# Token shift kept in a ring buffer, both mixes on VectorE, and two edits of placement, in a fused attention, channel-mix and gating kernel

## The chip, the cores and the metric

The kernel runs on one core of a Trainium2 chip. A core has five engines with a queue each: TensorE (PE, matmuls; PEld is its loading of weights), VectorE (DVE), ScalarE (ACT), GpSimd (POOL) and SyncE (SP), which here issues the DMAs. Each engine works through its own instructions in a fixed order and waits on semaphores for the others. The metric is the device time of one execution in microseconds (us), the median of several; smaller is better.

## The reference

Three layers follow one another on 4 batches of 1088 tokens and 128 channels; all arrays are float32.

```
a, b = S1 q, S2 q;  phi = outer(a, b)                 # linear attention, 4 heads, 64 features
x = (phi(q) @ (phi(k)^T v)) / (phi(q) @ sum(phi(k)) + 1e-6)

x_prev = x one token earlier, zeros first
xk = mu_k * x + (1 - mu_k) * x_prev                   # the key mix
xr = mu_r * x + (1 - mu_r) * x_prev                   # the receptance mix
x  = sigmoid(xr @ w_r) * (relu(xk @ w_k)**2 @ w_v)    # d_ff 1024

h = relu(x @ w_in);  u, v = halves of h (512 each)
v_n = (v - mean) / sqrt(var + 1e-6)
v_s = w_spatial @ v_n + b_spatial                     # 1088 x 1088, over tokens
out = (u * v_s) @ w_out
```

## The kernel before

A matmul at nearly full precision is made of three: each operand is split into a high part H (a copy by ScalarE in the type fp32r) and a low part L (a subtraction by VectorE or GpSimd), and `mm3` multiplies LH, HH and HL. So almost every tile costs a copy (line 134, `copy`) and a subtraction (line 137, `low`).

The program is one long list without loops on the chip. The tokens of a batch are cut into chunks of 384, 384 and 320 columns (`CH`), 12 chunks over the 4 batches. The channel mix runs over 12 x 8 = 96 blocks g, one for each chunk and each 128 of the 1024 hidden channels: `up(g)` (three matmuls into one of three PSUM banks, then a relu by ScalarE at L362), `sqsplit` one block later (square, by ScalarE at L382 or L394, VectorE at L370 or GpSimd at L365, and the split), and `down` four blocks later (`LAG`). `kind(g)` says which of the engines squares; from block 26 to 85 the kinds P and D take turns. A relu gets its buffer from a ring of six, `RA` (m2 to m7), up to block 88; a P block takes a second one for its square.

All other work is planned onto the blocks: `plan(g, fn)` puts a call behind block g. For chunk j these are the attention's `q_feat`, `q_turn`, `q_num` and `q_out` (which copies the new x into xT), then `prep` (the shift's difference by GpSimd at L318, the key mix by VectorE at L319, its split), mostly at block 8j-8, then `prep_r` (the receptance mix: ScalarE at L335, VectorE at L336, and its split), mostly at block 8j-6, then `receive` and `gate` at 8j-1 and 8j. The difference, the key mix and the receptance mix share one buffer, mx. For the first chunk `prep` takes x from PSUM and makes no difference. `late` and `behind` put a call behind named instructions of other calls, so that it isn't drawn forward.

From block 34 on, rows of the gating layer's v are computed as they come (`v_tile`), and `normalise(0, d)` splits them for the d-th 128 columns: into n0H and n0L (d = 0, at block 72), n1H and n1L (d = 1, at block 85, both by the list `VN`), and the rest at the end. The first spatial products, (d, c) for the columns d and the chunk c of output tokens, are run among the last blocks, from block 93 in steps of two (`EARLY`, `ES`, `EP`, order `ORD0`); eight more follow as units u = 4 to 11, and then come the other batches.

The spatial weights are read in 27 tiles, 9 for each chunk of columns. `wstep` converts the tile that has been loaded (a copy by ScalarE and a low part) and issues the load of the next into one of two staging buffers, st. The third chunk's loads may begin at block 96. In a unit, `WB` gives the number of steps that are spread over the unit's eight groups of matmuls, and the unit of the third chunk's first use, u = 8, needs all nine.

The order of each engine's instructions comes from a planner that lays out the list in time by its own estimates, so that an edit at one place can shift the order at others.

Of the kernel before, what the change touches and what calls it, by code (L numbers as in the profile page):

```python
# [11 lines left out]
AF = mybir.ActivationFunctionType  # L12
ALU = mybir.AluOpType
# [16 lines left out]
QD = 7  # L30
V0 = (74, 76, 78, 88)
VS = (34, 40, 43, 49, 55, 60, 63, 66, 69)
VN = (72, 85)
CONVP = (512,)
NWARM = 10
NFILL = 3
# [20 lines left out]
LAG = 4  # L57
WDVE = ((0, 1), (1, 2), (2, 1), (2, 2), (3, 1), (3, 2), (4, 0), (4, 2), (6, 0), (7, 0), (7, 1), (8, 2))
VD0 = 2
WB = (0, 0, 4, 7, 2, 4, 1, 0)  # L60
NB0 = 9
W1G = 69
W1N = 8
# [21 lines left out]
def attn_moe_gmlp(ctx: ExitStack, tc: tile.TileContext, qT, kT, va, st, wk, wv, wr, win, wout,  # L85
                  wT, wtail, btail, mu, ident, msk, out):
    nc = tc.nc
    TE, VE, SE, GE = nc.tensor, nc.vector, nc.scalar, nc.gpsimd
# [7 lines left out]
    def sb(tag, shape, dt=F32):  # L96
        uid[0] += 1
        return pool.tile(shape, dt, tag=tag, bufs=1, name=f"{tag}_{uid[0]}")
# [7 lines left out]
    def rot(*tags):  # L106
        i = count.get(tags, 0)
        count[tags] = i + 1
        return tags[i % len(tags)]

    def m(i):
        return f"m{i}"
# [7 lines left out]

    idn = sb("idn", [128, 128])
    mk = sb("mk", [128, 24])
    mus = sb("mus", [128, 4])
    half = sb("half", [128, 1])
    ebias = sb("ebias", [128, 1])
    warm = sb("warm", [128, 1])
# [6 lines left out]
    def copy(dst, src):  # L133
        return SE.activation(out=dst, in_=src, func=AF.Copy)  # L134

    def low(eng, L, src, H):
        return eng.tensor_tensor(out=L, in0=src, in1=H.bitcast(F32), op=ALU.subtract)  # L137
# [27 lines left out]
    def load64(src, H, L, o, n):  # L165
        raw = sb(f"w{rot(*[-x for x in CVT]) * -1}", [128, n, 2], I32)
        nc.sync.dma_start(out=flat(raw), in_=src[:, o:o + n].bitcast(I32))
        pending_raw.append((raw, n, H[:, o:o + n], L[:, o:o + n]))
# [12 lines left out]
    q_s, k_s, v_s, kbd, xTs, kps, qst = {}, {}, {}, {}, {}, {}, {}  # L181
# [123 lines left out]
    anchor, prep_L, xk_op = [None, None, None], [None, None], [None]  # L305
    RA = [m(i) for i in (2, 3, 4, 5, 6, 7)]
    RB = [m(i) for i in (2, 3, 4)]
    xks, sgs, sqs, vvs, hls = {}, {}, {}, {}, {}
    x_last = [None]

    def prep(i):
        b, c = divmod(i, 3)
        o, n = CH[c]
        xT = xTs[b]
        xp = xT[:, o:o + n]
        xk = d = sb("mx", [128, n])
        if i:
            GE.tensor_tensor(out=d, in0=xT[:, o + 1:o + 1 + n], in1=xp, op=ALU.subtract)  # L318
            VE.scalar_tensor_tensor(out=xk, in0=d, scalar=mus[:, 0:1], in1=xp, op0=ALU.mult, op1=ALU.add)  # L319
        else:  # L320
            px, a = first_x
            xk_op[0] = VE.scalar_tensor_tensor(out=xk, in0=px[:, :n], scalar=mus[:, 0:1], in1=a, op0=ALU.mult, op1=ALU.add)
        H, L = sb(m(11 + i % 2), [128, n], F32R), sb(m(13 + i % 2), [128, n], F32R)
        prep_L[1] = copy(H, xk)
        if not i:
            behind(prep_L[1:], copy, xT[:, 1:1 + n], px[:, :n])
        prep_L[0] = low(VE, L, xk, H)
        xks[i] = (H, L)

    def prep_r(i):  # L330
        b, c = divmod(i, 3)
        o, n = CH[c]
        xp = xTs[b][:, o:o + n]
        xr = sb("mx", [128, n])
        SE.activation(out=xr, in_=xp, func=AF.Copy, scale=mus[:, 3:4])  # L335
        VE.scalar_tensor_tensor(out=xr, in0=xTs[b][:, o + 1:o + 1 + n], scalar=mus[:, 1:2], in1=xr, op0=ALU.mult, op1=ALU.add)  # L336
        H, L = sb("xrH", [128, n], F32R), sb("xrL", [128, n], F32R)
        copy(H, xr)
        low(GE, L, xr, H)
        sgs[i] = (H, L)  # L340
# [207 lines left out]
    def spatial(b, d, c, fill, early=False):  # L548
        while not all((k, c) in done for k in range(NK + 1)):
            was = wi[0], len(pending_raw)  # L550
            wstep()
            assert was != (wi[0], len(pending_raw))
        Hs, Ls, T1, T2 = vnt[b, d]
        xH, xL = xsp[b]
        o, n = CH[c]
        cs, ds = slice(o, o + n), slice(128 * d, 128 * d + 128)
        pu = bank(7 if early else 3)[:, :n]
        mm3(pu, winH[:, ds], winL[:, ds], xH[:, cs], xL[:, cs], True, True)
        u = sb(UT if early else rot(m(0), m(1)), [128, n])
        SE.activation(out=u, in_=pu, func=AF.Relu)  # L560
        acc = bank(6 if early else rot(0, 1))[:, :n]
        for k in range(NK):
            mm3(acc, Hs[k], Ls[k], *wtile(k, c), k == 0, False, 0)
            if k == 6 and gout:
                gout.pop(0)()
            for fn in fill.get(k, ()):
                fn()
        TE.matmul(acc, lhsT=T2, rhs=wtile(NK, c)[1], start=False, stop=False)
        TE.matmul(acc, lhsT=T1, rhs=wtile(NK, c)[0], start=False, stop=True)
        VE.tensor_tensor(out=u, in0=acc, in1=u, op=ALU.mult)  # L570
        put_out(b, d, c, u, early)
# [269 lines left out]
    for n in range(NWARM):  # L841
# [8 lines left out]
                     in1=mk[:, 0:2 * NH].unsqueeze(2).to_broadcast([128, 2 * NH, 16]), op=ALU.mult)  # L850
# [32 lines left out]
    nc.sync.dma_start(out=idn, in_=ident)  # L883
    load64(*wseq[0])
    nc.sync.dma_start(out=mus[:, 0:2], in_=mu)
    GE.tensor_scalar(out=mus[:, 2:4], in0=mus[:, 0:2], scalar1=-1.0, scalar2=1.0, op0=ALU.mult, op1=ALU.add)
    load64(*wseq[1])
    load_k(1)
    load64(*wseq[2])
# [6 lines left out]
    def behind(anchors, fn, *a):  # L896
        with ExitStack() as es:
            for x in anchors:
                es.enter_context(tc.issue_after(x.ins))
            fn(*a)  # L900
# [36 lines left out]
    def plan(g, fn, *a):  # L937
        todo.setdefault(g, []).append(lambda: fn(*a))
# [57 lines left out]
    for j in range(NT):  # L996
        plan(VS[j] - 1, late, x_tile, j)
        plan(VS[j], late, v_tile, 0, j)
        plan(VS[j] + 1, late, v_rest)
    plan(VN[0], normalise, 0, 0)  # L1000
    for n, g in enumerate(V0):
        plan(g, late, xsplit, 0, n)
    plan(VN[1], late, normalise, 0, 1)
    plan(NI * NF, late, normalise, 0, 2)
    for n in range(8):
        plan(GL + GW + n, wstep)
    for n in range(W1N):
        plan(W1G + n, wstep)
# [20 lines left out]
    for u, (d, c) in enumerate(ORD0):  # L1029
        if u < EARLY:  # L1030
            continue
        fill = {}

        def add(k, fn, *a):
            fill.setdefault(k, []).append(lambda: fn(*a))

        for k in range(WB[u] if u < len(WB) else 0):
            add(k, wstep)
        if u == EARLY:
            add(0, behind, [x_last[0]], xsplit, 1)  # L1040
        for n, j in enumerate({5: (0, 1), 6: (2, 3), 7: (4, 5), 8: (6, 7)}.get(u, ())):
            add(2 + 3 * n, v_rest)
            add(2 + 3 * n, v_tile, 1, j)
        for k, fn, *a in W2.get(u, ()):
            if fn == "load":
                add(k, sums_load, *a)
            else:
                add(k, held, sums, *a)
        if u == 9:
            add(2, v_rest)  # L1050
            for n in (11, 12):
                add(4, quad_load, 1, 0, n)
        if u == 10:
            add(2, tails, 1, 0, vtail[:, 0])
            for n in (22, 21):
                add(2, quad_load, 1, 0, n)
        if u == 11:
            add(1, build, 1, 0, 0)
            add(4, build, 1, 0, 1)
        spatial(0, d, c, fill)  # L1060
# [100 lines left out]
```

## Time and profile before

| | before |
|---|---|
| median of 3 runs | 452.26 us (452.08 to 452.52) |
| the profiled execution, whole | 452.46 us |
| its span in the trace | 450.7 us |
| TensorE busy, share of the span | 440.8 us, 98% |
| VectorE, ScalarE, GpSimd busy | 297.5, 270.4, 223.2 us |

The span is what the trace covers; the execution's own time is 1.8 us longer. Busy times are sums over the span. Matmuls overlap in the pipe and their ends are modelled, so that PE's busy share is an upper measure; what counts is where its next matmul starts late.

### The profile page before, as it was taken

To read this page: it belongs to the slowest core of one execution; us is meant where nothing else is said; L and a number is where in the kernel's file an instruction comes from. 1 tells how busy PE (TensorE), PEld (TensorE's weight loads), DVE (VectorE), ACT (ScalarE), POOL (GpSimd) and SP (SyncE) were. 2 spreads that over 40 slices of the span, in tenths; PEclk is the share of its full clock that TensorE was granted. 3 is DMA by queue.
4 is the path that set the end of the run, shared out by engine and by line. 5 is a ranking of instruction groups with operands and counts; after the bars stand their busy time and mean duration, and the time that the engine had idled before them with its cause. 6 is when DMAs were issued, how large, how long until landed. Compare 5 with 4: busy or idle time off the path is not lost.

```text
span 450.7 us, 7621 instructions
## 1 busy us (share of the span) xinstructions
PE 440.8 (98%) x2691; PEld 420.4 (93%) x2691; DVE 297.5 (66%) x531; ACT 270.4 (60%) x629; POOL 223.2 (50%) x271
## 2 busy tenths in 40 slices
PE   8899999999999999999999999999999999999997
PEld 7897989989998988899999999999999999999996
DVE  5995777779864986566587797862755951734513
ACT  2595888998977898767446664334545434533322
POOL 2166477496744585868222426544435534335220
PEclk9999999999999999999999999999999999999999
DMA  7981100011100030033238422313022232010001
GB/s 232 369 297 49 51 0 2 2 52 54 27 2 0 22 120 19 19 87 113 59 117 256 131 63 93 118 54 110 15 85 93 72 110 69 19 41 25 0 2 49
DMA packets 30950, 34.92 MB, mean 77 GB/s; under 512 B 2816, under 2 KB 26432, under 8 KB 30912
## 3 DMA queue, kind: packets, MB, share of 16 engines
q1 hardware_dynamic: 30768, 34.43, 23.8%
q8 instruction: 21, 0.34, 0.3%
q14 instruction: 17, 0.14, 0.1%
q10 hardware_dynamic: 144, 0.01, 0.0%
HBM read 25.91 MB, written 8.52 MB: 76 GB/s over the span
## 4 chain that ended last, share of the span: by engine, by line
PE 84%; DVE 6%; DMA 3%; ACT 3%; POOL 1%; issue 1%; SPq 1%; ACTq 0%; DVEq 0%
PE p L131 67%; PE p L406 5%; PE p L276 3%; PE p L239 2%; PE p L208 2%; DMA w<-in_wk_dram 1%; PE p L260 1%; PE p L722 1%; PE p L721 1%; DMA st<-in_wT_dram 1%; DVE w L148 1%; DVE w L147 1%; PE p L294 1%; ACT m L362 1%; DVE mx L319 1%
## 5 line engine op out<-in xcount | busy, mean ns | idle before, releaser
L131 PE MATMUL p<-m,k 128*128 128x384 f32 (+1 forms) x288 | 65.5, 349 | 0.0
L131 PE MATMUL p<-w,k 128*128 128x384 f32 (+1 forms) x360 | 63.8, 323 | 0.0
L131 PEld LDWEIGHTS p<-w,k 128*128 128x128 f32 x360 | 59.2, 188 | 0.3
L621 DVE TENSOR_TENSOR m<-p,m 128x384 f32<-128x384 f32 (+2 forms) x37 | 18.6, 520 | 57.0 <-PE p L722 56.1
L134 ACT ACTIVATE m<-m 128x384 fp32r<-128x384 f32 (+2 forms) x49 | 24.6, 502 | 45.9 <-DVE m L735 25.6
L131 PEld LDWEIGHTS p<-m,k 128*128 128x128 f32 x288 | 48.2, 189 | 4.1
L137 POOL TENSOR_TENSOR k<-VR,k 128x512 fp32r<-128x512 f32 x25 | 34.0, 1364 | 33.4 <-ACT k L134 28.6
L362 ACT ACTIVATE m<-p 128x384 f32<-128x384 f32 (+1 forms) x96 | 43.1, 468 | 8.2 <-PE p L131 6.4
L137 DVE TENSOR_TENSOR m<-m,m 128x384 fp32r<-128x384 f32 (+1 forms) x48 | 34.3, 715 | 11.2 <-ACT m L134 8.8
L131 PE MATMUL p<-w,n1H 128*128 128x384 f32 (+1 forms) x192 | 41.1, 326 | 0.0
L365 POOL TENSOR_TENSOR m<-m 128x384 f32<-128x384 f32 (+1 forms) x35 | 30.0, 859 | 21.5 <-ACT m L362 21.0
L137 DVE TENSOR_TENSOR w<-m,w 128x384 fp32r<-128x384 f32 (+1 forms) x35 | 26.0, 746 | 15.4 <-POOL m L365 11.4
L131 PE MATMUL p<-w,n1L 128*128 128x384 f32 (+1 forms) x168 | 34.8, 324 | 0.9 <-POOL n1L L137 0.9
L134 ACT ACTIVATE m<-p 128x384 f32<-128x384 f32 (+1 forms) x36 | 17.1, 482 | 30.0 <-PE p L131 21.7
L137 POOL TENSOR_TENSOR n1H<-VR,n1H 128x512 fp32r<-128x512 f32 x12 | 15.5, 1293 | 37.1 <-ACT n1H L134 26.4
L406 PE MATMUL p<-w,wvT 128*128 128x384 f32 (+1 forms) x86 | 33.4, 470 | 0.0
L131 PEld LDWEIGHTS p<-w,n1H 128*128 128x128 f32 x192 | 32.6, 188 | 0.5
L500 POOL TENSOR_SCALAR rs<-mv 128x1 f32<-128x1 f32 x34 | 8.8, 260 | 43.3 <-DVE mv L499 42.4
L131 PEld LDWEIGHTS p<-w,n1L 128*128 128x128 f32 x168 | 28.5, 188 | 1.4 <-POOL n1L L137 1.2
L504 DVE TENSOR_SCALAR VR<-VR,mv,rs 128x512 f32<-128x512 f32 x24 | 20.5, 855 | 12.6 <-POOL rs L501 12.3
L134 ACT ACTIVATE k<-VR 128x512 fp32r<-128x512 f32 x25 | 15.7, 630 | 21.4 <-PE p L131 17.1
L131 PE MATMUL p<-w,xs1H 128*128 128x384 f32 (+1 forms) x90 | 26.9, 338 | 0.0
(288 smaller groups left out, 1212.6 us busy)
## 6 DMA issues: line engine op xcount, KB each, us to landing
vd<-VR SPq DMA_DIRECT2D x24, 256.0 KB, 2.0
VR<-vd SPq DMA_DIRECT2D x24, 256.0 KB, 2.9
st<-in_wT_dram SPq DMA_DIRECT2D x16, 192.0 KB, 2.4
w<-in_kT_dram SPq DMA_DIRECT2D x8, 192.0 KB, 4.4
w<-in_qT_dram SPq DMA_DIRECT2D x8, 192.0 KB, 4.0
VR<-in_wT_dram SPq DMA_DIRECT2D x8, 192.0 KB, 2.6
out_dram<-m SPq DMA_DIRECT2D x8, 192.0 KB, 2.1
m<-in_wT_dram SPq DMA_DIRECT2D x8, 192.0 KB, 4.5
```

The costliest lines, as they stand in the source:

```text
L131: TE.matmul(out_ap, lhsT=l, rhs=r, start=first and n == 0, stop=last and n == 2, skip_group_check=skip)
L134: return SE.activation(out=dst, in_=src, func=AF.Copy)
L137: return eng.tensor_tensor(out=L, in0=src, in1=H.bitcast(F32), op=ALU.subtract)
L208: TE.matmul(wide[:, 64 * t:64 * t + 128], lhsT=src[:, cut(c, t, CH[c][0])], rhs=Sbd, start=True, stop=True)
L239: TE.matmul(kv[:, w * g:w * g + w], lhsT=kp, rhs=vt if wide else vt[:, VP * g:VP * g + VP], start=(t == 0), stop=(t == NT - 1))
L276: nd_pe[0] = TE.matmul(o.rearrange("p h c -> p (h c)"), lhsT=qt[g][:, cut(c, t)], rhs=kb[:, g], start=not wide or g == 0, stop=not wide or ...
L362: SE.activation(out=r, in_=hk, func=AF.Relu)
L365: anchor[2] = GE.tensor_tensor(out=sq, in0=r, in1=r, op=ALU.mult)
L406: TE.matmul(vvs[i], lhsT=wvT[:, f // 2], rhs=hls.pop(g), start=f == 0, stop=f == NF - 1)
L500: GE.tensor_scalar(out=rs, in0=mv[:, 1:2], scalar1=1e-6, scalar2=None, op0=ALU.add)
L504: VE.tensor_scalar(out=v, in0=r, scalar1=mv[:, 0:1], scalar2=rs, op0=ALU.subtract, op1=ALU.mult)
L621: return eng.tensor_tensor(out=o, in0=a, in1=b_, op=op)
```

## The change

The difference x - x_prev gets a buffer of its own, from the relus' ring (m0 for the first chunk), and stays there until the receptance mix is made. Both mixes are then one VectorE instruction each, from the difference: xk = mu_k * d + x_prev and xr = mu_r * d + x_prev. ScalarE's scaling by 1 - mu_r goes. The first chunk's difference is a new GpSimd instruction behind the copy of its x. `normalise(0, 1)` moves from block 85 to block 83. The steps at blocks 96 to 99 go; in the units, `WB` now names the groups of matmuls behind which a step stands: the 2nd, 5th and 8th of units 4, 5 and 6, and the 2nd and 5th of unit 7. Before, it was one step behind each of the first 2 groups of unit 4, the first 4 of unit 5 and the first of unit 6.

```
-VN = (72, 85)
+VN = (72, 83)
...
-WB = (0, 0, 4, 7, 2, 4, 1, 0)
+WB = {4: (1, 4, 7), 5: (1, 4, 7), 6: (1, 4, 7), 7: (1, 4)}
...
-    mus = sb("mus", [128, 4])
+    mus = sb("mus", [128, 3])
...
     def prep(i):
...
-        xk = d = sb("mx", [128, n])
+        d = ds_[i] = sb(rot(*RA) if i else m(0), [128, n])
+        xk = sb("mx", [128, n])
         if i:
             GE.tensor_tensor(out=d, in0=xT[:, o + 1:o + 1 + n], in1=xp, op=ALU.subtract)
             VE.scalar_tensor_tensor(out=xk, in0=d, scalar=mus[:, 0:1], in1=xp, op0=ALU.mult, op1=ALU.add)
...
         if not i:
             behind(prep_L[1:], copy, xT[:, 1:1 + n], px[:, :n])
+            GE.tensor_tensor(out=d, in0=xT[:, o + 1:o + 1 + n], in1=xp, op=ALU.subtract)
...
     def prep_r(i):
...
         xr = sb("mx", [128, n])
-        SE.activation(out=xr, in_=xp, func=AF.Copy, scale=mus[:, 3:4])
-        VE.scalar_tensor_tensor(out=xr, in0=xTs[b][:, o + 1:o + 1 + n], scalar=mus[:, 1:2], in1=xr, op0=ALU.mult, op1=ALU.add)
+        VE.scalar_tensor_tensor(out=xr, in0=ds_.pop(i), scalar=mus[:, 1:2], in1=xp, op0=ALU.mult, op1=ALU.add)
...
-    GE.tensor_scalar(out=mus[:, 2:4], in0=mus[:, 0:2], scalar1=-1.0, scalar2=1.0, op0=ALU.mult, op1=ALU.add)
+    GE.tensor_scalar(out=mus[:, 2:3], in0=mus[:, 0:1], scalar1=-1.0, scalar2=1.0, op0=ALU.mult, op1=ALU.add)
...
-    for n in range(8):
+    for n in range(4):
         plan(GL + GW + n, wstep)
...
-        for k in range(WB[u] if u < len(WB) else 0):
+        for k in WB.get(u, ()):
             add(k, wstep)
```

(`GL + GW` is 92, so that the steps of the second last edit stood at blocks 92 to 99 and stand at 92 to 95.)

## Rows read from the trace of the kernel before

**Rows 1.** Windows: stretch, length, PE, PEld, DVE, ACT, POOL, clock, DMA, GB/s.

```profile
160.00:182.00 22.00, 21.03 (x109) 18.45 (x108) 16.13 (x24) 19.50 (x50) 15.27 (x17) 1.00 0.21 63
182.00:204.00 22.00, 21.34 (x127) 20.55 (x126) 13.28 (x21) 15.05 (x38) 14.74 (x17) 1.00 0.21 58
204.00:240.00 36.00, 36.00 (x202) 34.90 (x202) 24.62 (x49) 19.19 (x45) 15.67 (x24) 1.00 0.34 109
```

**Rows 2.** Timeline of PE: start, length, work, [idle before, its releaser].

```profile
42.54 0.52 PE L294 MATMUL p<-idn,VR 128*128 128x128 f32 x3 [0.41 <-DVE VR L282]
...
65.30 1.17 PE L131 MATMUL p<-m,k 128*128 128x320 f32 x6
67.14 0.39 PE L131 MATMUL p<-w,xs1L 128*128 128x320 f32 x1 [0.66 <-DVE de L281]
...
180.12 0.55 PE L131 MATMUL p<-w,n1H 128*128 128x384 f32 x2
181.57 0.44 PE L131 MATMUL p<-w,n1L 128*128 128x384 f32 x1 [0.91 <-POOL n1L L137]
...
202.64 0.45 PE L131 MATMUL p<-m,xs1H 128*128 128x320 f32 x2
203.76 0.81 PE L406 MATMUL p<-m,wvT 128*128 128x320 f32 x2 [0.66 <-ACT m L382]
...
210.00 3.81 PE L131 MATMUL p<-w,k 128*128 128x384 f32 x21
213.64 0.33 PE L131 MATMUL p<-xrH,woL 128*128 128x384 f32 x1
```

**Rows 3.** Waits of PE: line, releaser, us in total, times, longest.

```profile
PE p L260 <- DVE n1L L219: 0.3, 1, 0.3
```

**Rows 4.** The chain that ended last, around 175 to 181 us: start, us, what.

```profile
175.06 1.11 DVE mx L319
...
179.47 0.53 ACT n1H L134
...
180.06 1.46 POOL n1L L137
```

**Rows 5.** Timeline of ScalarE.

```profile
168.90 0.47 ACT L134 ACTIVATE xs0H<-x 128x320 fp32r<-128x320 f32 x1
...
185.56 0.24 ACT L134 ACTIVATE xs0H<-x 128x64 fp32r<-128x64 f32 x1
...
199.66 0.47 ACT L134 ACTIVATE w<-st 128x320 fp32r<-128x320 f32 x1 [1.26 <-DMA st<-in_wT_dram]
...
201.29 0.47 ACT L134 ACTIVATE w<-st 128x320 fp32r<-128x320 f32 x1 [0.43 <-DMA st<-in_wT_dram]
201.66 0.42 ACT L362 ACTIVATE m<-p 128x320 f32<-128x320 f32 x1
202.87 0.47 ACT L134 ACTIVATE w<-st 128x320 fp32r<-128x320 f32 x1 [0.79 <-DMA st<-in_wT_dram]
...
216.05 0.47 ACT L134 ACTIVATE w<-st 128x320 fp32r<-128x320 f32 x1 [2.69 <-DMA st<-in_wT_dram]
```

**Rows 6.** Timeline of VectorE, 62 to 67 us.

```profile
62.01 0.62 DVE L336 SCALAR_TENSOR_TENSOR mx<-x,mus,mx 128x384 f32<-128x384 f32 x1 [0.74 <-ACT mx L335]
...
66.91 0.21 DVE L281 RECIPROCAL de<-de 128x12 f32<-128x12 f32 x1
```

**Rows 7.** Tile mx: count, ns min/median/max, first and last start, forms.

```profile
L335 ACT ACTIVATE mx<-x,mus x12: 552/608/630, 41.5 to 177.7; 128x384 f32<-128x384 f32 x8, 128x320 f32<-128x320 f32 x4
L336 DVE SCALAR_TENSOR_TENSOR mx<-x,mus,mx x12: 544/608/770, 42.3 to 178.3; 128x384 f32<-128x384 f32 x8, 128x320 f32<-128x320 f32 x4
...
L318 POOL TENSOR_TENSOR mx<-x x11: 716/823/1271, 37.5 to 174.3; 128x384 f32<-128x384 f32 x7, 128x320 f32<-128x320 f32 x4
L319 DVE SCALAR_TENSOR_TENSOR mx<-mx,mus,x x11: 528/1165/1844, 38.3 to 175.1; 128x384 f32<-128x384 f32 x7, 128x320 f32<-128x320 f32 x4
```

**Rows 8.** Timeline of GpSimd, first instruction after the start-up's idle time.

```profile
26.48 1.57 POOL L137 TENSOR_TENSOR w<-m,w 128x384 fp32r<-128x384 f32 x1 [7.80 <-PE p L260]
```

More of the change, by code (lines that the diff above doesn't have):

```diff
@@ L32 @@
 VS = (34, 40, 43, 49, 55, 60, 63, 66, 69)
-VN = (72, 85)
+VN = (72, 83)
 CONVP = (512,)
@@ L59 @@
 VD0 = 2
-WB = (0, 0, 4, 7, 2, 4, 1, 0)
+WB = {4: (1, 4, 7), 5: (1, 4, 7), 6: (1, 4, 7), 7: (1, 4)}
 NB0 = 9
@@ L122, in attn_moe_gmlp @@
     mk = sb("mk", [128, 24])
-    mus = sb("mus", [128, 4])
+    mus = sb("mus", [128, 3])
     half = sb("half", [128, 1])
@@ L307, in attn_moe_gmlp @@
     RB = [m(i) for i in (2, 3, 4)]
-    xks, sgs, sqs, vvs, hls = {}, {}, {}, {}, {}
+    xks, sgs, sqs, vvs, hls, ds_ = {}, {}, {}, {}, {}, {}
     x_last = [None]
@@ L315, in prep @@
         xp = xT[:, o:o + n]
-        xk = d = sb("mx", [128, n])
+        d = ds_[i] = sb(rot(*RA) if i else m(0), [128, n])
+        xk = sb("mx", [128, n])
         if i:
@@ L326, in prep @@
             behind(prep_L[1:], copy, xT[:, 1:1 + n], px[:, :n])
+            GE.tensor_tensor(out=d, in0=xT[:, o + 1:o + 1 + n], in1=xp, op=ALU.subtract)
         prep_L[0] = low(VE, L, xk, H)
@@ L334, in prep_r @@
         xr = sb("mx", [128, n])
-        SE.activation(out=xr, in_=xp, func=AF.Copy, scale=mus[:, 3:4])
-        VE.scalar_tensor_tensor(out=xr, in0=xTs[b][:, o + 1:o + 1 + n], scalar=mus[:, 1:2], in1=xr, op0=ALU.mult, op1=ALU.add)
+        VE.scalar_tensor_tensor(out=xr, in0=ds_.pop(i), scalar=mus[:, 1:2], in1=xp, op0=ALU.mult, op1=ALU.add)
         H, L = sb("xrH", [128, n], F32R), sb("xrL", [128, n], F32R)
@@ L885, in attn_moe_gmlp @@
     nc.sync.dma_start(out=mus[:, 0:2], in_=mu)
-    GE.tensor_scalar(out=mus[:, 2:4], in0=mus[:, 0:2], scalar1=-1.0, scalar2=1.0, op0=ALU.mult, op1=ALU.add)
+    GE.tensor_scalar(out=mus[:, 2:3], in0=mus[:, 0:1], scalar1=-1.0, scalar2=1.0, op0=ALU.mult, op1=ALU.add)
     load64(*wseq[1])
@@ L1004, in attn_moe_gmlp @@
     plan(NI * NF, late, normalise, 0, 2)
-    for n in range(8):
+    for n in range(4):
         plan(GL + GW + n, wstep)
@@ L1035, in add @@
             fill.setdefault(k, []).append(lambda: fn(*a))
-        for k in range(WB[u] if u < len(WB) else 0):
+        for k in WB.get(u, ()):
             add(k, wstep)
```

## The prediction

> **What bounds the kernel now.** I read the table of windows first. TensorE (PE) is the bound nearly everywhere: in the 36 us from 204 us on it is busy all of the time, and in the two 22 us windows before that it is short of full by 0.97 and 0.66 us, at full clock [rows 1]. So time can be won only where PE stands still, and the sum below counts those places alone. The timeline of PE marks each pause with its length and with what ended it. Behind the start-up there are three that cost over 0.6 us by their brackets: at 67.14, 181.57 and 203.76 us [rows 2]. The bracket counts from the modelled end of the last matmul, so I reckon the loss from start to start. Twenty-one matmuls of 384 columns take 213.64 - 210.00 = 3.64 us, 0.173 us each [rows 2]; 320 columns are then 0.144 us. Loss at 67: 67.14 - 65.30 - 6 x 0.144 = 0.98 us. At 181: 181.57 - 180.12 - 2 x 0.173 = 1.10 us. At 204: 203.76 - 202.64 - 2 x 0.144 = 0.83 us. Together 2.91 us; the smaller pauses, as the 0.3 us in PE's list of waits [rows 3], come on top.
>
> Next, who is late at each. The chain of waits shows that the pause at 181 ends with GpSimd (POOL) writing n1L, behind ScalarE's n1H at 179.47, and that ScalarE's run of work goes back to VectorE's mix at 175.06 [rows 4]. That is the normalise call for the second rows, placed at block 85. The pause at 204 is ended by a Square of ScalarE (L382). The timeline of ScalarE shows why it was late: in front of it stand three copies of the third weight chunk, each waiting for its DMA, 1.26, 0.43 and 0.79 us, and the relu on which that Square works stands among them at 201.66 [rows 5]. The pause at 67 is ended by VectorE, which had itself sat idle 0.74 us for ScalarE's scaling at L335 before the receptance mix at 62.01 [rows 6].
>
> **The change part by part.**
>
> A, normalise at block 83. Between the split at block 78 (168.90) and the one at block 88 (185.56) a block takes 1.67 us [rows 5], so two blocks are 3.3 us. n1L's first half (1.46 us) would then end near 181.5 - 3.3 = 178.2 [rows 4], while PE is ready for it at 180.47. It takes the work of two 512-wide copies and their differences along, nothing is added. The whole 1.10 us goes, if PE has no other late operand there. Bounds: 0 to 1.10 gained; I take 1.10, since the margin is 2.2 us. The work that now yields is ScalarE's and POOL's squares of blocks 83 and 84; they are read by the matmuls four blocks later (LAG), 6.7 us, which covers it. Without that cover it costs what it gains.
>
> B, third weight chunk. Of nine third-chunk tiles, three were converted at blocks 97 to 99, the others in units 4 and 5 as fast as the steps came. Now the steps at blocks 96 to 99 are gone, and units 4, 5 and 6 convert three each, three matmul groups apart (the two steps in unit 7 find nothing to do). From ScalarE's queue ahead of 203.76 go the three copies with 2.48 us of waits in front of them [rows 5]; the relu and its Square move up by as much, three times the pause, so it goes whole, also if the first copy of unit 4 should be drawn forward with a wait of its own. Bounds 0 to 0.83; I take 0.83. The loads (SP's queue) move with the conversions. Between a load and its conversion there are three groups of three matmuls, 9 x 0.173 = 1.6 us, short beside the waits of the copies in [rows 5], so ScalarE will wait in the units too. That is hidden: in the kernel before a copy in the units waited 2.69 us at 216.05 [rows 5] and PE was busy 36.00 of 36 us, with ScalarE at 19.19 [rows 1]. Unit 8 is the first reader, one whole unit after the last conversion. One conversion of the second chunk, the bias rows' tile, slips from block 96 to 97, 1.67 us, and is read last in its unit. Cost 0. If SP's queue, where stores of the value rows and loads of the sums now stand between these loads, held them for over a unit, unit 8 would wait.
>
> C, mixes on VectorE alone. Twelve ScalarE operations go, median 608 ns [rows 7]; ScalarE's and not PE's time. VectorE keeps its twelve scalar_tensor_tensor, with the same two SBUF inputs and form, so it gets no new work. What counts is the pause at 67: the receptance mix no longer waits for ScalarE (0.74 us idle, [rows 6]), and from there its timeline has no pause up to the reciprocal at 66.91, which released PE [rows 6]. The subtraction, too, no longer waits for the one buffer mx. So of 0.98 us I take 0.74; bounds 0 and 0.98.
>
> D, what C costs. The shift of the first chunk is a new POOL operation, median 823 ns [rows 7]. POOL stood idle 7.80 us until 26.48 [rows 8], and the first x is there well before; cost 0, at most 0.82 where it runs late or holds VectorE up. The receptance mix of the first chunk can now run ahead of the reciprocal and the product (L282) for which PE already waits 0.41 us at 42.54 [rows 2]: 0.61 us (the median of L336, [rows 7]) if it does, 0 if not. I take half, 0.30.
>
> E, the ring. Each of eleven shifts takes one of the relus' six buffers. A relu with its square takes three buffers in two blocks, so a buffer comes round in four blocks, 6.7 us. The shift holds it from prep to prep_r, two blocks, 3.3 us, and, if VectorE is late by its longest mix, 1.84 us more [rows 7]: 5.2 of 6.7 us. Cost 0, with 1.5 us to spare. The constant with one column less, made by POOL once at the start, is nothing.
>
> Sum: 1.10 + 0.83 + 0.74 - 0.30 = 2.37 us. The profiled execution took 452.46, so 450.09; it stands 0.2 above the median of the runs, and from that, 452.26, the sum gives 449.9. I forecast 450.0.
>
> **A rule weighed.** The mix at L319, started just behind POOL's subtraction, took 528 to 1844 ns with a median of 1165; L336, the same form at another moment, 608 [rows 7]. So a mix is nearly twice as dear when it starts at a wrong time. The Trainium skill, "SBUF — State Buffer", section "SBUF: two separate sides", says that a VectorE operation with two SBUF inputs and a GpSimd operation that reads SBUF exclude each other for the whole of an instruction; the spread of these rows agrees with it. By that rule, the second mix, freed from ScalarE, could be drawn next to POOL's work too, which is the second rival.
>
> **The rivals.**
>
> 1. Slower: the ring is too short. If prep_r's mix comes over 1.5 us later than reckoned under E, the relu that gets its buffer waits in ScalarE's queue, the PSUM bank with it, and PE stops. From 0.32 us at each of eleven chunks (2.67 gained under A, B and C, and 0.9 to spare for slower) it decides; at 0.41, the size of the pause at 42.54 [rows 2], the time is 452.3 - 2.67 + 4.5 = 454.1. For it: VectorE is busy 16.1 of 22 us around 170 [rows 1]. Against: the mix only loses a wait. Chance 0.08; other ways to slower, mainly a start-up held up by D's bounds in the new order with A or B failing, 0.05.
>
> 2. The mix collides: 0.56 us more in L336 (1165 - 608). Where it leads to PE (near 67) C falls from 0.74 to 0.18: 452.3 - 1.10 - 0.83 - 0.18 + 0.30 = 450.5. All twelve on PE's path would be 6.7 us, but nearly everywhere VectorE is ahead. Chance 0.12.
>
> 3. The normalise pause moves: squares behind n1H and n1L are then late instead, and A gives nothing: 452.3 - 0.83 - 0.74 + 0.30 = 451.0; with C gone as well 451.7. Chance 0.15, two thirds of it above 451.3.
>
> 4. Nothing comes of it: the order of the engines' instructions is planned anew from start to end, and new small pauses like that of [rows 3], some seven of them, use up the gain: 452.0. Chance 0.08.
>
> **How the numbers follow.** The forecast, with 449.1 to 451.2 around it, has 0.52. The bound of what can be told from no change is 0.2%, 0.9 us, here 451.36 and 453.16. Faster: 0.52 + 0.12 + a third of 0.15 = 0.69. Same: 0.10 + 0.08 = 0.18. Slower: 0.13. The range runs from 449.0, where D costs nothing and small pauses go as well, to 452.3, which takes in rivals 2, 3 and 4 and leaves rival 1 out, some 0.15 in all.
>
> **What would show it.** In the new trace: no pause of PE for n1L, and n1L's first half written before 179 (A); no copy of a third-chunk tile on ScalarE before PE's first unit of the third rows, and no wait of the last down matmuls for L382 (B); VectorE's receptance mix straight behind the low part of the key mix, and the pause near 67 below 0.3 us (C); the first shift before 24 us and no longer pause near 42 (D); no wait of L362 for the receptance mix (E). Wrong would be: a relu waiting for a buffer, PE waiting for w or m behind n1L, or new pauses between 30 and 70 us that sum to over 1 us.

## The result, and the profile after

The changed kernel takes 454.87 us (median of four runs, 454.29 to 455.42), against 452.17 us for the kernel before beside it: a ratio of 1.0058, with a 95% interval of 1.0040 to 1.0075. The forecast was 450.0 us, faster; the kernel is slower by 2.6 us (from the ratio; 2.7 between the medians). The profiled execution took 454.29 us, its span is 452.5 us.

The page's busy times, and the three windows that answer to [rows 1]:

```profile
PE 442.5 (98%) x2691; PEld 421.5 (93%) x2691; DVE 300.8 (66%) x531; ACT 265.5 (59%) x617; POOL 223.5 (49%) x272
```

```profile
160.00:182.00 22.00, 20.69 (x110) 18.14 (x108) 16.29 (x25) 17.05 (x42) 13.59 (x16) 1.00 0.21 63
182.00:204.00 22.00, 21.86 (x126) 20.50 (x126) 13.62 (x20) 16.46 (x41) 16.81 (x19) 1.00 0.18 54
204.00:240.00 36.00, 36.00 (x203) 34.95 (x202) 23.99 (x50) 18.98 (x45) 15.57 (x24) 1.00 0.32 102
```

ScalarE has lost its twelve scalings (629 operations before, 617 now) and 4.9 us of work. In the window from 182 us PE has gained half a microsecond; in the window ahead of it PE has lost 0.34 us, at a granted clock of 1.00 in each. The timeline of PE (start, length, work, then in brackets the idle time ahead and its releaser), to be laid beside [rows 2], shows that the pauses have changed places:

```profile
42.11 0.52 PE L294 MATMUL p<-idn,VR 128*128 128x128 f32 x3 [0.62 <-DVE VR L282]
...
67.32 0.71 PE L131 MATMUL p<-m,k 128*128 128x320 f32 x3 [0.26 <-DVE m L371]
71.68 0.94 PE L239 MATMUL p<-xs0H,n0H 128*128 128x132 f32 x6 [0.68 <-ACT x L134]
94.10 0.50 PE L131 MATMUL p<-winH,w 128*128 128x512 f32 x1 [0.44 <-DVE w L137]
105.97 0.94 PE L208 MATMUL p<-Sbd,w 128*128 128x128 f32 x6 [0.78 <-DVE n1L L219]
...
173.42 1.31 PE L131 MATMUL p<-m,k 128*128 128x384 f32 x6 [0.67 <-ACT m L134]
175.37 0.79 PE L131 MATMUL p<-m,k 128*128 128x384 f32 x3 [0.64 <-ACT m L363]
```

The pauses at 181 and 204 us are gone and the one near 67 has shrunk from 0.66 to 0.26 us by its bracket. In their place stand pauses at 71.68, 94.10, 105.97, 173.42 and 175.37, which the kernel before doesn't have, together 3.21 us by their brackets. So the question is what made these.

**Who waits for the ring.** The timeline of GpSimd, VectorE and ScalarE at two places (the line numbers stand one higher than before: the shift is L319, the key mix L320, the receptance mix L337, the relu L363, GpSimd's square L366):

```profile
57.75 1.00 POOL L137 TENSOR_TENSOR w<-m,w 128x384 fp32r<-128x384 f32 x1 [2.76 <-ACT w L134]
58.83 0.82 POOL L319 TENSOR_TENSOR m<-x 128x384 f32<-128x384 f32 x1
...
170.90 1.50 POOL L319 TENSOR_TENSOR m<-x 128x384 f32<-128x384 f32 x2 [1.66 <-ACT x L134]
...
173.99 0.62 DVE L337 SCALAR_TENSOR_TENSOR mx<-m,mus,x 128x384 f32<-128x384 f32 x1
...
174.76 0.82 POOL L366 TENSOR_TENSOR m<-m 128x384 f32<-128x384 f32 x1 [2.35 <-PE p L131]
...
175.62 0.48 ACT L363 ACTIVATE m<-p 128x384 f32<-128x384 f32 x1
...
179.81 0.55 DVE L337 SCALAR_TENSOR_TENSOR mx<-m,mus,x 128x320 f32<-128x320 f32 x1
...
180.50 0.83 POOL L366 TENSOR_TENSOR m<-m 128x384 f32<-128x384 f32 x1 [2.42 <-DVE mx L337]
```

Two shifts run together at 170.90, for the last two chunks. Each keeps a buffer of the relus' ring until its receptance mix has read it, and GpSimd's square, whose buffer is that one, starts 0.14 us after the receptance mix's end both times (173.99 + 0.62 = 174.61; 179.81 + 0.55 = 180.36). GpSimd stood still for 2.35 and 2.42 us ahead of it. The first bracket names PE, since that event came late too; the buffer's last reader is L337. The relu at 175.62 in turn starts 0.04 us after that square's end, 174.76 + 0.82, since it gets the buffer that the square has read.

The shift at 58.83 shows the other side: it gets the buffer of a relu written at 55.88, whose last reader is the low part at 57.75, and stands behind that. So the ring makes squares wait for shifts, a relu wait behind such a square, and shifts wait for relus. The last is a way by which it can reach PE: the key mix, the receptance mix and what PE does with them come after the shift (the experiments with a longer ring come back to it). The pause at 71.68 can be followed along it:

```profile
63.80 1.15 DVE L337 SCALAR_TENSOR_TENSOR mx<-m,mus,x 128x384 f32<-128x384 f32 x1
...
67.19 0.21 DVE L281 RECIPROCAL de<-de 128x12 f32<-128x12 f32 x1
67.51 1.19 POOL L137 TENSOR_TENSOR xrL<-mx,xrH 128x384 fp32r<-128x384 f32 x1
68.74 1.62 DVE L320 SCALAR_TENSOR_TENSOR mx<-m,mus,x 128x384 f32<-128x384 f32 x1 [0.44 <-POOL xrL L137]
70.45 0.52 ACT L134 ACTIVATE m<-mx 128x384 fp32r<-128x384 f32 x1 [0.62 <-DVE mx L320]
...
71.20 0.43 ACT L134 ACTIVATE x<-p 128x320 f32<-128x320 f32 x1
```

The receptance mix of the late shift starts at 63.80. Its low part xrL comes at 67.51, behind other work of GpSimd, and both mixes share the buffer mx, so that the next key mix waits for xrL. ScalarE waits for that mix, and the copy of x for which PE waits at 71.68 stands behind in its queue. The pause at 94.10 is not the ring's alone: e7, e9 and e13 below have one of 0.39 to 0.62 us near there too. What makes the one at 105.97 stays open. The two pauses at 173 and 175 us, though, do not come from a wait for the ring: PE's turning of the new x at 169.81 and its copy at 170.33 stand ahead of the shift at 170.90.

Joining the writer of each ring buffer with its last reader and its next writer, over the whole trace up to 186 us, gives how long a buffer is held and how soon its next writer starts (us; where that writer had to wait, the wait is in the figure):

```
                       held: median, longest    next writer after: median, shortest
before  relu           1.90   6.59              7.65   3.75
before  GpSimd square  2.22   4.04              6.64   2.90
after   shift          5.95   8.68              8.82   3.85
after   relu           1.90   9.08              7.08   1.84
```

**The mixes.** The tile's own rows (count, shortest, median and longest ns):

```profile
L337 DVE SCALAR_TENSOR_TENSOR mx<-m,mus,x x12: 541/706/1844, 40.6 to 179.8; 128x384 f32<-128x384 f32 x8, 128x320 f32<-128x320 f32 x4
...
L320 DVE SCALAR_TENSOR_TENSOR mx<-m,mus,x x11: 530/1052/1622, 37.5 to 177.3; 128x384 f32<-128x384 f32 x7, 128x320 f32<-128x320 f32 x4
```

The longest receptance mix was 770 ns before [rows 7] and is 1844 now; the key mix's median fell from 1165 to 1052.

### The profile page after: what moved, and what is told of

The parts are those of the page before. It is cut to its first block, busy times and chain, and to the rows that moved or that the text cites. A ratio compares the mean times of both kernels' runs of the same rounds, so it can differ in the third digit from the quotient of the medians.

```text
span 452.5 us, 7594 instructions
## 1 busy us (share of the span) xinstructions
PE 442.5 (98%) x2691; PEld 421.5 (93%) x2691; DVE 300.8 (66%) x531; ACT 265.5 (59%) x617; POOL 223.5 (49%) x272
## 4 chain that ended last, share of the span: by engine, by line
PE 78%; DVE 10%; POOL 3%; ACT 3%; issue 2%; DMA 1%; SPq 1%; ACTq 0%; POOLq 0%; DVEq 0%
PE p L131 66%; PE p L407 4%; PE p L276 2%; DMA w<-in_wk_dram 1%; DVE w L148 1%; PE p L723 1%; PE p L722 1%; ACT m L363 1%; DVE w L147 1%; DVE mx L337 1%; PE p L208 1%; DVE mx L320 1%; PE p L239 1%; PE p L260 1%; DVE w L144 1%
## 5 line engine op out<-in xcount | busy, mean ns | idle before, releaser
L131 PE MATMUL p<-m,k 128*128 128x384 f32 (+1 forms) x288 | 68.2, 354 | 2.1 <-ACT m L134 0.7
L363 ACT ACTIVATE m<-p 128x384 f32<-128x384 f32 (+1 forms) x96 | 43.8, 468 | 12.1 <-PE p L131 8.4
L366 POOL TENSOR_TENSOR m<-m 128x384 f32<-128x384 f32 (+1 forms) x35 | 29.1, 830 | 25.1 <-ACT m L363 20.0
L137 DVE TENSOR_TENSOR w<-m,w 128x384 fp32r<-128x384 f32 (+1 forms) x35 | 27.4, 785 | 19.6 <-POOL m L366 14.9
```

Source lines behind the costliest of these rows:

```text
L131: TE.matmul(out_ap, lhsT=l, rhs=r, start=first and n == 0, stop=last and n == 2, skip_group_check=skip)
L363: SE.activation(out=r, in_=hk, func=AF.Relu)
L366: anchor[2] = GE.tensor_tensor(out=sq, in0=r, in1=r, op=ALU.mult)
```

## The experiments

All times are medians beside runs of the kernel before on the same chip; ratios are to that kernel, with 95% intervals. 1% is 4.5 us. Lines are those of each kernel's own text.

**Which part costs? e1 to e4.** The change is the sum of three edits that can be made one by one: `VN` (A), `WB` with the steps at blocks 96 to 99 (B), and the mixes' part (C, D, E). e1 has A and B, e2 the mixes' part alone, e3 A alone, e4 B alone.

```
 e3:  VN = (72, 83)
 e4:  WB = {4: (1, 4, 7), 5: (1, 4, 7), 6: (1, 4, 7), 7: (1, 4)}  and  for n in range(4): plan(GL + GW + n, wstep)
 e1:  both;  e2: the rest of the change, with VN and WB of before
```

> The two placements alone (normalise at block 83, third weight chunk in the units), the mixes as in the kernel before. Theory M (the mixes' part costs all that was lost, by late operands between 40 and 110 us and at 173 and 175 us; the placements gain): 452.2 - 1.1 - 0.8 = 450.3, with no pause at 181 and 204. Theory N (normalise at 83 crowds out the work that feeds the blocks, as the new pauses at 173 and 175 suggest by their place): 453 or more, with pauses of PE between 170 and 185 of over 1.5 us.

> The mixes' part alone (shift in the ring, both mixes on VectorE), both placements as before. Theory M: 454.9 + 1.9 = 456.8 if the pauses of normalise and of the third chunk come back, 454.9 if their places in the new order are harmless; pauses between 40 and 110 us and at 173 and 175 as in the changed kernel. Theory N: 451.5 to 452.5, no pause at 173.

> Normalise at block 83 alone. Theory M: 452.2 - 1.1 = 451.1, the pause at 181 gone, the one near 204 there. Theory N: 453 or more.

> The third weight chunk in the units alone. Both theories: 452.2 - 0.8 = 451.4, the pause at 181 there and the one at 204 gone; PE without a pause in the units.

Measured: e1 452.02 us, 0.9989 (0.9980 to 0.9997); e2 457.36, 1.0108 (1.0090 to 1.0125); e3 452.04, 0.9989 (0.9981 to 0.9998); e4 452.22, 0.9995 (0.9985 to 1.0004). The mixes' part costs all of it, and more. The theory that the normalise call crowds something out falls. But A and B together give 0.5 us where 1.93 was reckoned. Why A gives so little is in GpSimd's timeline of e3, beside [rows 4]:

```profile
180.49 1.59 POOL L137 TENSOR_TENSOR n1L<-VR,n1H 128x512 fp32r<-128x512 f32 x1
182.05 1.29 POOL L137 TENSOR_TENSOR n1L<-tt,n1H 128x512 fp32r<-128x512 f32 x1
```

The tile is no earlier than before (180.06); PE's first product with it now starts at 182.44 in place of 181.57, so the pause has gone because PE has other work first. The call moved in the list, the work didn't move on its engine. Why B gives nothing, ScalarE's timelines show. First the kernel before, with a fourth copy beside the three of [rows 5], then e1:

```profile
197.61 0.47 ACT L134 ACTIVATE w<-st 128x320 fp32r<-128x320 f32 x1
...
203.25 0.45 ACT L382 ACTIVATE m<-m 128x320 f32<-128x320 f32 x1
```

```profile
197.19 0.47 ACT L134 ACTIVATE w<-st 128x320 fp32r<-128x320 f32 x1 [0.38 <-DMA st<-in_wT_dram]
...
199.06 0.47 ACT L134 ACTIVATE w<-st 128x320 fp32r<-128x320 f32 x1 [0.39 <-DMA st<-in_wT_dram]
...
200.90 0.47 ACT L134 ACTIVATE w<-st 128x320 fp32r<-128x320 f32 x1 [0.42 <-DMA st<-in_wT_dram]
...
202.36 0.47 ACT L134 ACTIVATE w<-st 128x320 fp32r<-128x320 f32 x1 [0.67 <-DMA st<-in_wT_dram]
202.74 0.45 ACT L382 ACTIVATE m<-m 128x320 f32<-128x320 f32 x1
```

Before and in e1 alike, four copies of 320-wide tiles stand ahead of the Square L382; their waits for DMAs are 2.48 us before and 1.86 in e1. The planner draws the units' conversions forward, since nothing holds them. The changed kernel has four as well, and its Square starts later than before; the pause is gone there because PE's product with it stands later in the order:

```profile
203.18 0.47 ACT L134 ACTIVATE w<-st 128x320 fp32r<-128x320 f32 x1 [1.14 <-DMA st<-in_wT_dram]
...
204.14 0.47 ACT L134 ACTIVATE w<-st 128x320 fp32r<-128x320 f32 x1 [0.16 <-DMA st<-in_wT_dram]
204.51 0.46 ACT L383 ACTIVATE m<-m 128x320 f32<-128x320 f32 x1
...
205.52 0.70 PE L407 MATMUL p<-m,wvT 128*128 128x320 f32 x2
```

**Ring, or mixes? e5 to e8.** All four have A and B. m8 and m9 lie idle until block 88, so that a shift can have them. e5 gives the shift these and keeps both mixes on VectorE; e6 keeps the ring and gives the receptance mix back to ScalarE and VectorE; e7 does both; e8 is e1 with the receptance call of every chunk but the first one block later, an edit of order alone.

```
 e5:      d = ds_[i] = sb(rot(m(8), m(9)), [128, n])
 e6:      d = sb(rot(*RA), [128, n]) if i else None
 e7:      d = sb(rot(m(8), m(9)), [128, n]) if i else None
 e6, e7:  SE.activation(out=xr, in_=xp, func=AF.Copy, scale=mus[:, 3:4])
          VE.scalar_tensor_tensor(out=xr, in0=xTs[b][.. one later ..], scalar=mus[:, 1:2], in1=xr, ...)
 e8:      plan(max(8 * j - 5, e + 3), prep_r, j)        # in place of 8 * j - 6, e + 2
```

> The changed kernel with the shift in two buffers of its own (m8 and m9, idle until block 88), not in the relus' ring. Theory R (the ring is short by the slot that the shift holds): 452.0, like the two placements alone. Theory X (the mixes on VectorE, without ScalarE's step in between, meet GpSimd's work and come late): 454.9 as the changed kernel. Theory O (any edit of the mixes makes the planner lay out a new order, and the constants fit the old one alone): anything from 452 to 457, with other pauses than in the changed kernel.

> The changed kernel with the receptance mix as before (ScalarE scales, VectorE adds), the shift still in the ring but free again after the key mix; no shift for the first chunk. Theory R: between 452 and 454.9, since the slot is held for a shorter time. Theory X: 452.0, with VectorE's receptance mix at a median near 608 ns. Theory O: anything from 452 to 457.

> As the run before, and the shift in m8 and m9. Theories R and X: 452.0. Theory O: anything from 452 to 457.

> The two placements with the mixes as in the kernel before, and prep_r planned one block later (8j-5 and e+3): the same instructions and buffers, another place in the list. Theories R and X: 452.0, within 0.5. Theory O: over 453, with new pauses between 30 and 110 us.

Measured, with e1 and the changed kernel for the whole square:

```
                          receptance by ScalarE + VectorE       by VectorE alone
difference in mx          e1  452.02  0.9989                    -
difference in m8, m9      e7  451.58  0.9972 (0.9960-0.9984)    e5     453.59  1.0017 (1.0006-1.0029)
difference in the ring    e6  454.74  1.0054 (1.0036-1.0071)    after  454.87  1.0058 (1.0040-1.0075)
e8: 452.24, 0.9991 (0.9979-1.0003)
```

The ring costs 3.2 us with ScalarE's mix and 1.3 with VectorE's; VectorE's mix costs 2.0 us with buffers of its own and nothing that can be told in the ring. The costs don't add: they depend on which of the two is there already. By the ratios, the way over e6 is +0.82% for the ring and +0.04% for the mix, the way over e5 +0.45% for the mix and +0.41% for the ring. That any new order costs time falls with e8, one edit of order that costs nothing that can be told. Still, in each of these kernels the planner's order differs too, so that what is shown is the cost of a part together with the order that goes with it. e7 beats both kernels.

**Is it the ring's length? e9, e10, e13.** e9 is e6 with a ring of eight, m2 to m9: the same buffers as e7, shared out otherwise. e13 is the changed kernel with that ring. e10 is the reverse: e1, which has no shift in the ring, with a ring of five.

```
 e9, e13:  RA = [m(i) for i in (2, 3, 4, 5, 6, 7, 8, 9)]
 e10:      RA = [m(i) for i in (2, 3, 4, 5, 6)]
```

> As e6 (both placements, shift taken from the relus' ring, receptance mix by ScalarE and VectorE as before, no shift for the first chunk), but the ring has eight buffers, m2 to m9, in place of six. It has the same buffers as e7, only shared out in another way. Theory S (the ring of six is too short for relus, squares and shifts together, so that calls stand later in the order and relus wait): as e7, 451.3 to 452.0 us. Theory P (that the shift takes turns with the relus, and so where the allocations fall, costs the time, whatever the ring's length): near e6's 454.7.

> As e1 (both placements, old mixes in mx), but the relus' ring has five buffers, m2 to m6, in place of six: the reverse test, a buffer fewer with no shift in the ring. TensorE's order is that of e1 in its first 590 rows or so. Theory S (the relus need nearly all of the ring): a buffer lost for good costs at least what the shift costs, 454 to 457 us. Theory P: five are enough, 451.8 to 452.6 us, as e1's 452.02.

> The changed kernel with one edit: the relus' ring has eight buffers, m2 to m9, in place of six. Theory S (a shift sits in a buffer of the ring for 5.95 us in the median and 8.68 at most, so squares and relus behind it in the ring's turn wait): the ring's part goes and what the mixes by VectorE cost stays, as e5: 453.3 to 453.9 us; POOL's two waits of 2.4 us for the receptance mix at 174.8 and 180.5 us are gone. Theory P (the ring is no cause of its own in the kernel as changed): 454.6 to 455.2 us.

Measured: e9 452.19 us, 0.9998 (0.9987 to 1.0010), 0.56% under e6; e13 453.51, 1.0024 (1.0015 to 1.0033), 0.34% under the changed kernel, and at e5's time; e10 452.89, 1.0005 (0.9993 to 1.0017). In the changed kernel two buffers more take the ring's cost away. Beside the old mix they take 0.56 of its 0.82%; against e7, which has the same eight buffers shared out otherwise, 0.26% stay, and the intervals don't meet. In e13's GpSimd timeline no square waits for a mix, and the shift that stands at 58.83 us in the changed kernel runs here, ahead of the work it stood behind there:

```profile
51.83 0.82 POOL L319 TENSOR_TENSOR m<-x 128x384 f32<-128x384 f32 x1 [0.52 <-DVE mx L337]
```

(It waits 0.52 us for the mix of the chunk before, whose shift had the same buffer.) The chunk's mixes are late or early with it. Start of this chunk's shift and of its receptance mix in each kernel (us), with the time that PE loses between 60 and 110 us (from the table under e12):

```
             ring of six        own buffers       ring of eight     mx
            after     e6       e5       e7       e9      e13      before
shift       58.8     59.7     51.1     51.0     50.2     51.8      57.3
mix         63.8     66.9     57.9     60.1     59.3     58.1      62.0
PE loses     3.50     3.39     1.22     1.09     1.57     1.41      1.74
```

The ring of six holds this shift up by some 8 us, and in the stretch behind it PE loses about 2 us more. That this chunk alone makes the 2 us is not shown: in the kernel before it is nearly as late, behind the last use of mx, with a smaller loss.

e10 corrects the theory on one point. A buffer lost for good costs 0.16% (0.7 us, not clear of nothing by the intervals), far from the 2 us and more that was expected, though a shift takes a buffer only part of the time. So that five buffers are left is not what costs most. The ring is given out in turn, and a shift that holds its buffer for 5.95 us, against 1.90 for a relu (medians), stops the turn when it comes to that buffer, whether others are free or not. In e6 the shift is given back at the key mix, after 2.51 us in the median, and the same happens in another place: a second shift at 61.82 us waits for the first to be read:

```profile
59.72 0.82 POOL L319 TENSOR_TENSOR m<-x 128x384 f32<-128x384 f32 x1
61.82 0.82 POOL L319 TENSOR_TENSOR m<-x 128x384 f32<-128x384 f32 x1 [1.28 <-DVE mx L320]
```

That the turn and not the count decides is argued from e10, these rows and e9 against e7; no run changed the turn alone.

**The mixes' 2.0 us. e12.** Up to 45 us e5's trace has VectorE's receptance mixes as the changed kernel has them, 0.6 us later. In the changed kernel, VectorE and GpSimd around 42 us:

```profile
40.61 0.62 DVE L337 SCALAR_TENSOR_TENSOR mx<-m,mus,x 128x384 f32<-128x384 f32 x1
41.15 0.22 DVE L281 RECIPROCAL de<-de 128x12 f32<-128x12 f32 x1
41.41 0.56 DVE L282 TENSOR_TENSOR VR<-p,de 128x384 f32<-128x384 f32 x1
...
42.83 1.51 POOL L219 TENSOR_TENSOR n1L<-sab 128x768 f32<-128x768 f32 x1
...
42.91 1.84 DVE L337 SCALAR_TENSOR_TENSOR mx<-m,mus,x 128x384 f32<-128x384 f32 x1 [0.94 <-POOL xrL L137]
```

The first chunk's mix has gone ahead of the reciprocal (D's fear), and the second's runs beside GpSimd's n1L and takes 1.84 us in place of 0.62 (rival 2's). The Trainium skill, "SBUF — State Buffer", section "SBUF: two separate sides", has the two exclude each other for a whole instruction. The mix, begun 0.08 us after n1L, ends 0.41 us after it, which agrees with a wait, though less than its 0.62 us are left behind n1L. e12 moves the receptance calls of e5 one block later, as e8 did with the old mixes: all but the first chunk's.

> As e5 (the change with m8 and m9 for the shift, both mixes by VectorE), but the receptance mix's call stands one block later for every chunk, which cost nothing with the old mixes (e8 against e1: 452.24 and 452.02). Theory X1 (the mixes by VectorE cost by their moment: the receptance mix, freed from ScalarE, runs ahead of the reciprocal and the product and beside POOL's work): another moment, another time, 451.6 to 452.8 us, and the pauses of e5 between 40 and 70 us go or shrink. Theory X2 (VectorE's mixes are dear wherever they stand): 453.4 to 454.0 us.

Measured: 452.32 us, 1.0005 (0.9996 to 1.0015). So by the ratios e12 is 0.12% (0.5 us) under e5, by the medians 1.3 us, and the intervals overlap. Against e7, with the same buffers and the old mixes, it is 0.33% (1.5 us) slower, clear of the intervals; against e8, 0.6 us, which the intervals don't separate from nothing. Its partner, e7 with the call one block later, was not run. So how much of the 2.0 us hangs on the moment stays open. And what goes does not go where the theory said: in e12 the first chunk's mix still runs ahead of the reciprocal (41.09 and 41.62 us) and the second's still takes 1.84 us beside n1L (43.38). The table sums, over PE's matmuls in each stretch, how much later each began than is usual in these runs after the same neighbours (us, from 20 us on):

```
us        20-40   40-60   60-80  80-110 110-160 160-190 190-210 210-240
before     0.58    1.55    1.20    0.54    0.17    1.99    1.03    0.15
after      0.11    1.73    1.55    1.95    0.25    3.02    0.12    0.21
e5         0.57    2.06    1.20    0.02    0.19    3.10    0.11    1.40
e6         0.13    1.52    1.75    1.64    0.22    3.48    0.10    0.35
e7         0.57    1.74    0.06    1.03    0.14    2.37    0.11    0.16
e9         0.14    1.52    0.54    1.03    0.20    2.16    0.09    0.19
e11        0.10    1.23    1.22    0.53    0.17    1.63    0.09    0.18
e12        0.56    1.90    0.69    0.07    0.18    1.48    2.15    0.16
e13        0.58    1.97    0.26    1.15    0.18    2.12    1.20    0.20
```

Each row is one profiled execution; e5's (454.24 us) is 0.65 us above its median, so that e5 and e7 differ by 2.5 us here. Up to 160 us e5 loses 4.04 us and e7 3.54: a net 0.5 us, in which the colliding mixes and the early one are contained. The rest lies at 160 to 190 us (0.7) and in one pause in the units (1.2). That pause, in ScalarE's and PE's timeline of e5, stands at one of the conversions that B spreads over the units:

```profile
210.93 0.94 ACT L134 ACTIVATE w<-st 128x320 fp32r<-128x320 f32 x2 [2.03 <-DMA st<-in_wT_dram]
214.87 0.47 ACT L134 ACTIVATE w<-st 128x320 fp32r<-128x320 f32 x1 [3.00 <-DMA st<-in_wT_dram]
215.25 0.47 ACT L561 ACTIVATE m<-p 128x384 f32<-128x384 f32 x1
...
215.77 0.44 PE L131 MATMUL p<-xs0H,winL 128*128 128x384 f32 x1 [0.99 <-ACT m L561]
```

A conversion waits 3.00 us for its load, the copy L561 waits behind it in the queue, and PE waits for that. So in these two executions it is mostly in the last blocks and units that the kernel with VectorE's mixes loses. Which instruction sets that order stays open.

**The conversions held. e11, e14, e15.** e11 is e1 with each third-chunk conversion put behind `x_last`, VectorE's multiplication that follows the last down matmul; e14 is e12 with the same tie, e15 is e7 with it.

```
-        behind([x for x in anchor[:2] if x is not None and pending_raw[0][1] == 0], wconv)
+        behind([... as before ...] + ([x_last[0]] if pending_raw[0][1] == 2 else []), wconv)
```

> As e1 (both placements, old mixes), but each conversion of the third weight chunk is held behind the last matmul of the down products, so that none can be drawn ahead of the Square of L382. Theory B1 (the copies of the third chunk ahead of that Square make the pause at 203 us, 0.5 us by its bracket in e1): no pause there, 451.4 to 451.6 us. Theory B2 (what is held up then comes too late in the units, or another operand is late at once): 451.9 to 452.8 us, with a pause of PE between 205 and 230 us.

> e12 (own buffers m8 and m9 for the shift, both mixes by VectorE, receptance mix one block later) with the third chunk's conversions held behind the last down matmul, as in e11. If the three causes found add up (ring 1.28 us, moment of the receptance mix 1.3 us, conversions ahead of L382 0.6 us, as medians against their partners): 452.3 less 0.6 to 1.3, since e12 loses 2.15 us between 190 and 210 us: 451.0 to 451.7 us, faster than the kernel before by 0.1 to 0.3%. If what is held up comes too late in this order: 452.3 us or more.

> e7 (own buffers m8 and m9 for the shift, receptance mix by ScalarE and VectorE as before, both placements) with the third chunk's conversions held behind the last down matmul. e7 has next to no loss left between 190 and 210 us (0.11 us from start to start, after 1.03 in the kernel before), so by theory B1 (the hold pays only where those copies make PE wait) it changes nothing: 451.2 to 451.9 us. If the hold pays or costs by itself: under 450.9, or over 452.2 us.

Measured: e11 451.41 us, 0.9979 (0.9967 to 0.9991); e14 453.46, 1.0018 (1.0004 to 1.0032); e15 452.17, 0.9992 (0.9982 to 1.0003). The tie did not do what was meant: it held only the part of a conversion that is VectorE's own. In e11 three of ScalarE's copies (196.65, 198.41 and the one below) still pass ahead of the Square. VectorE's two low parts run at 202.98, behind that multiplication at 202.57, so the staging buffers come free later, and the fourth copy waits for its load until 208.88. With three copies in place of four the Square starts earlier, and the loss from 190 to 210 us falls from 0.84 (e1) to 0.09 us:

```profile
200.37 0.47 ACT L134 ACTIVATE w<-st 128x320 fp32r<-128x320 f32 x1 [0.61 <-DMA st<-in_wT_dram]
200.75 0.42 ACT L362 ACTIVATE m<-p 128x320 f32<-128x320 f32 x1
201.20 0.47 ACT L382 ACTIVATE m<-m 128x320 f32<-128x320 f32 x1
```

So the profile shows B's mechanism: with one copy fewer ahead of the Square the pause is gone. As time it is 0.10% against e1, and the intervals overlap. That the causes add up is not shown: e14 was expected at 451.0 to 451.7 and is slower than e12, by 0.13% (their intervals overlap). Its profile has the gain (1.63 in place of 2.15 us lost from 190 to 210) and a new loss of 1.4 us from 240 to 300; e15, expected at 451.2 to 451.9 and 0.20% above e7, has one of 1.9 there, where e12 and e7 have 0.3 and 0.5. In e15 it is a wait for a split in the second batch:

```profile
274.23 0.47 ACT L134 ACTIVATE m<-m 128x320 fp32r<-128x320 f32 x1 [3.27 <-DVE m L622]
...
274.76 0.41 PE L131 MATMUL p<-m,woL 128*128 128x320 f32 x1 [0.66 <-ACT m L134]
```

e11, with the same tie, has no such pause, so the tie alone is not its cause; what is stays open. Of all kernels that ran, e7 and e11 are the fastest, 0.2 to 0.3% under the kernel before.

## Why the prediction was wrong, step by step

The forecast failed at two steps above all, **E**, costed at nothing, and **C**, forecast as a gain. Together with D they were to gain 0.44 us; measured against e1, with A and B alone, they cost 0.69% (3.1 us).

**E**, 0: its terms were a turn of 6.7 us and a hold of 5.2 with "1.5 us to spare". Measured: a hold of 5.95 us in the median and 8.68 at most. The planner runs the shift as soon as x and a buffer are there, not at block 8j-8, and the next writer came after 8.82 us in the median but 3.85 at its shortest. One reckoned hold was set against one reckoned turn; relus, squares and shifts don't come evenly. At 174.76 a square waits although the shift ahead of it held the buffer for only 3.71 us, under the 5.2; GpSimd had stood idle for 2.35 us of that. The ring costs 1.3 to 1.9 us in the changed kernel (against e5 and e13, by medians and by ratios) and 3.2 to 3.7 beside the old mix (e6 against e7). This was **rival 1**, at 0.08. It had the ring right and the waiting in part: it saw relus wait at each of eleven chunks, with PE behind them. In the trace no relu waits for a shift itself; two of GpSimd's squares do, one relu behind one of them, and shifts wait for relus. That its 454.1 us lies near the result is luck, since it kept the gains of A, B and C whole. "Against: the mix only loses a wait" was the wrong ground: the mix's own wait has nothing to do with how early the shift is made.

**C**, 0.74 us: the pause near 67 went from 0.66 to 0.26 us by its bracket, under the 0.3 that was to show it, but not by the step forecast. The receptance mix was to come earlier and with it the reciprocal that released PE; it starts at 63.80 in place of 62.01, behind the late shift, and the reciprocal at 67.19 in place of 66.91. PE now waits there for another operand (m, L371), and from 60 to 80 us it loses 1.55 us in place of 1.20. "VectorE gets no new work" failed too: its busy time rose from 297.5 to 300.8 us, as the receptance mix's median from 608 to 706 ns and its longest from 770 to 1844. With buffers of its own for the shift, VectorE's mixes cost 2.0 us (e5 against e7); why is open in the main, since the stretches up to 160 us hold a net 0.5 us of it. The prediction looked at one pause only.

**D**, 0.30 us: near the forecast. The first shift runs at 20.81 us, 1.00 us long, in GpSimd's idle time. Of the 0.61 us that were to come or not, half was taken; it came, the mix stands ahead of the reciprocal, and the pause at 42 grew from 0.41 to 0.62 us.

**A**, 1.10 us: the pause went, but 0.5 us was all it gave (e3). The step "n1L's first half would then end near 178.2" failed: it ends at 182.08 in e3 and 186.00 in the changed kernel, later than before. A call's block is a place in a list, not a time.

**B**, 0.83 us: nothing by itself (e4), because "from ScalarE's queue go the three copies" failed: the same four copies stand there in e1 and in the changed kernel as before. The pause at 204 is missing in the changed kernel, as in e7, because PE has other work first. And "Cost 0" in the units holds only in some orders; in e5 a conversion costs 1.2 us at 215.77. With the mixes' part A and B are worth 0.5% (e2 against the changed kernel), by another order than the one reckoned with.

**Rival 2** is there too: the collisions are seen, as at 42.91, within the 0.5 us up to 160. **Rival 4**, a new order that uses up the gain, is part of it at 160 to 216 us, though an edit of order alone (e8) costs nothing. **Rival 3** is not: e3 is not slower for its moved squares.

The sum by measured parts, as differences of ratios: A and B -0.11% (e1), buffers of their own for the shift -0.17% (e7 to e1), VectorE's mixes +0.45% (e5 to e7), the ring +0.41% (the changed kernel to e5): +0.58%, the ratio measured. The last two change places by the other way: the ring +0.82% (e7 to e6), the mixes +0.04%.

## What to carry to other kernels

Before a long-lived value is put into a ring of short-lived ones, set its longest hold, from the earliest moment its writer can run to its last reader, against the shortest turn of the ring, not an average against an average: the cost shows as writers that start just as the buffer's last reader ends, the long-lived value's own writer among them. Where a planner sets the order, a call that is moved in the list may leave its instructions where they were; what must come later needs a tie to what it is to follow, and one that reaches each engine's share: e11's held VectorE's alone. A pause that disappears is no proof of the step that was to remove it; look at whether the late operand came earlier. And a two-step operation shared by two engines can be cheaper than the one-step form, here by 0.45% (e7 against e5), for a reason that is open in the main.

## What the runs showed of the hardware

The same VectorE instruction, a 128x384 mix from two SBUF operands, took 0.62 us at 40.61 and 1.84 us at 42.91, where it ran beside a GpSimd operation of 1.51 us; in e12 and e13, too, the longest took 1.84 and 1.85 us. In the changed kernel's trace, 12 of the 23 mixes that read the difference run beside a GpSimd operation on two SBUF operands of 320 to 768 columns that has begun before them (or, at 103.48, 0.03 us after). All 12 end 0.41 or 0.42 us (384 columns) or 0.35 us (320 columns) after that operation, and so took 0.79 to 1.84 us. The other 11 took 0.53 to 0.62 us. So here a collision cost what was left of GpSimd's operation, less some 0.2 us. And what a wait for a load costs depended on what was queued behind it: ScalarE waited 2.69 us for a staging buffer before at no loss [rows 5], and in e5 3.00 us, with the copy L561 next in its queue, and PE lost 0.99.
